# Folding the forward sequence transform of a spectral block about the middle of each tile's rows

## The chip, the cores and the metric

The kernel runs on one core of a Trainium2 chip. A core has five engines that each work through their own instructions in program order: TensorE (PE) multiplies matrices, VectorE (DVE), ScalarE (ACT) and GpSimd (POOL) work element by element, and SyncE (SP) mainly starts transfers. Transfers are also started by ACT and POOL. The metric is the device time of one execution in microseconds, the median of several runs; smaller is better. What is profiled is one execution on the chip.

## The reference

The input x is (1, 2048, 1024): S = 2048 positions and D = 1024 channels. The layer-normed x goes two ways, and the results are combined:

```python
def _A_ref(x, w_r, w_i):
    X = rfft2(x, axes=(-2, -1))
    X = X * (w_r + 1j * w_i)            # (2048, 513)
    return irfft2(X, (S, D), axes=(-2, -1))

def _B_ref(x, w1, w2):                  # w1 (1024, 3584), w2 (3584, 1024)
    h = _silu(einsum("bsd,df->bsf", x, w1))
    return einsum("bsf,fd->bsd", h, w2)

xn = _layernorm(x)
return x + _A_ref(xn, w_r, w_i) * _silu(_B_ref(xn, w1, w2))
```

## The kernel before

**Numbers.** Every product is made of float16 halves: a value is scaled and split into a high half (`high`, on ACT) and the rest (`low`, on DVE), and three matmuls (high by high, high by low, low by high) add up in PSUM.

**Two streams on PE.** The feed-forward network fills PE: 112 chunks of 24 matmuls (`pa`, line 466, 128x512 each) for the first product, then 56 chunks of 42 (`pb`, lines 549 to 551) for the second, in which seven products of halved size stand for the whole. After each `pa` chunk and each half of a `pb` chunk, `work()` lets one or more steps of a list of background jobs run; the spectral path is cut into such steps. An estimated clock for PE and one for DVE decide how many steps run, so that DVE stays near PE. The order on every engine is fixed when the program is built.

**The spectral path.** In order: `ln_gen` (layer norm), `fd_gen(c)` for c = 0 to 3 (the transform over D for the rows s = 4a + c, then a radix step over S), a switch of memory pools, `f_gen` (forward transform over S, the product with W, the first inverse radix step), a second switch, and `i_gen(c)` for c in the order 1, 3, 0, 2 (the inverse over S and D). The jobs up to the first switch are forced to their end when 15 `pa` chunks are left. A value `s` of the column sums (line 266) scales each pair of w1 blocks: PE multiplies the maxima `m1b`, which POOL casts to bfloat16 (line 290), with a tile of ones, DVE makes the scale `rs` out of it, and ACT and DVE split w1 with that.

**fd_gen, second half.** `vt` (named `V` in the trace) holds the transform over D of one c. For each j of four column blocks DVE adds and subtracts (`Rb`, `Rd`, lines 900 and 901) and makes the radix step (`radix4`, lines 244 to 247) into `Ro`; a sum `total` (line 909, called `vt` in the trace) is added; ACT and DVE split both into `Rs` (lines 884, 886, 889, 890), and SP stores them two chunks later to the DRAM tiles `vd[j]` (512 KB) and `vs[j]` (128 KB). One j is one step; the steps end two after the fourth.

**f_gen.** For 16 units u = (q, j), SP loads `vq` out of `vd[j]` (line 966, 512 KB), the weights `wq`, and for q = 2, 3 `vs`. `kq` holds the twiddle planes of a q, three for each c (cosine and both signs of the sine, or the three of a three-product complex multiplication), 768 KB; it is loaded by POOL for q = 0 and by ACT else. `mat(u)` is the product on PE, called `fx` in the trace: for q = 0, 1, in each of 12 groups, one 128x256 matmul and two of 128x128 (lines 1001 to 1003); for q = 2, 3, 36 of 128x128 (line 994) in two PSUM tiles, and DVE then adds the planes (two adds). Then DVE makes the radix step, the product with W and the next radix step.

**i_gen.** Per c, products over S (`iu`), radix or mirror steps on DVE, products back over D (`id`, line 1372), and on DVE the rows of s, `rows` (lines 1385 to 1419). The end of the kernel adds the pieces: `pl` (lines 618 and 619), times s, plus x (lines 633 and 634), out by SP; `fx` on SP is there the load of x rows, not the product.

**Queues.** SP carries nearly all loads and stores, in order. A pool switch (`close`) writes out all deferred stores, and the first tiles in the freed memory wait for everything that used it.

Of the kernel before, what the change touches and what calls it, by code (L numbers as in the profile page):

```python
# [14 lines left out]
I32 = mybir.dt.int32  # L15
AF = mybir.ActivationFunctionType
# [11 lines left out]
THREE = (2, 3)  # L28
# [9 lines left out]
RH = math.sqrt(0.5)  # L38
EPS = 1e-5
# [8 lines left out]
def make_constants():  # L48
# [9 lines left out]
    ca = np.stack(_halves(ca, 2.0**14), 1)  # L58

    q = np.arange(4)[:, None, None, None]  # L60
    a = np.arange(128)[None, :, None, None]
    c = np.arange(4)[None, None, :, None]
    m1 = np.arange(128)[None, None, None, :]
    th = 2 * np.pi * (((4 * a + c) * (4 * m1 + q)) % 2048) / 2048
    k = np.stack([-np.sin(th), np.cos(th), np.sin(th)], 3)
    k[list(THREE)] = np.stack([np.cos(th), np.sin(th) - np.cos(th), -np.sin(th) - np.cos(th)], 3)[list(THREE)]
    kc = np.stack(_halves(k, 2.0**14), 3).reshape(4, 128, 3072)
# [5 lines left out]
    for c in (0, 2):  # L73
        th = 2 * np.pi * (((4 * a + c) * (4 * row + q)) % 2048) / 2048
# [3 lines left out]
        if c == 0:  # L78
            re[..., 0:64], re[..., 64:127], re[..., 127], re[..., 128] = co[..., near], si[..., far], -si[..., 64], co[..., 64]
            im[..., 0], im[..., 1], im[..., 2:65], im[..., 65:129] = co[..., 64], si[..., 64], -si[..., far], co[..., near]  # L80
# [8 lines left out]
    for c in (1, 3):  # L89
        th = 2 * np.pi * (((4 * a + c) * (8 * half + 4 * e + q)) % 2048) / 2048  # L90
# [32 lines left out]
    tw = np.tile(tw[None], (128, 1)).astype(np.float32)  # L123
# [9 lines left out]
def spectral_ffn(ctx, tc, x, w_r, w_i, w1, w2, ca, kc, ci, tw, pm, out):  # L133
    nc = tc.nc
# [5 lines left out]
    kf = [kc[q][:, 0:3072].rearrange("a (c h t m) -> a c h t m", c=4, h=2, t=3) for q in range(4)]  # L140
    ki = [kc[c][:, 3072:5136] for c in range(4)]
# [12 lines left out]
    vs = [dp.tile([128, len(THREE), 4, 2, 128], F16, name=f"vs{j}") for j in range(4)]  # L154
# [12 lines left out]
    ones = cp.tile([128, 128], F32, name="ones")  # L167
    unit = cp.tile([128, 128], BF16, name="unit")
# [64 lines left out]
    def radix4(sign, b, d, o):  # L233
# [9 lines left out]
        sw = d[:, 1, ::-1]  # L243
        sub(o[:, 0:2], b[:, 0], b[:, 1], op=OP.add)
        sub(o[:, 4:6], b[:, 0], b[:, 1], op=OP.subtract)
        sub(pick(plus), d[:, 0], sw, op=OP.add)
        sub(pick(minus), d[:, 0], sw, op=OP.subtract)
# [568 lines left out]
    def fd_gen(c):  # L816
# [77 lines left out]
        for j in range(4):  # L894
            sl = slice(128 * j, 128 * j + 128)
            if j:
                high_r(j - 1)
# [818 lines left out]
```

## Time and profile before

| | |
|---|---|
| median of 3 runs | 1224.8 us (1223.97 to 1225.43) |
| span of the profiled execution | 1222.1 us, 19140 instructions |
| TensorE clock granted | 1.00 throughout |
| spectral forward part on the chip | radix steps of c = 0 from 142 us, of c = 3 to 523 us; `fx` from 551.5 us |

The profile's page gives for each engine its busy time and its share of the span. The views used below are the instructions in time order on an engine (start, duration, line, operation, output and inputs, and in brackets the idle time before and what ended it), a table of busy time per stretch of the span, and the list of transfers (count, size, median time from issue to landing). The span is 2.7 us shorter than the median of the runs.

### The profile page before, as it was taken

To read this page: it belongs to the slowest core of one execution; us is meant where nothing else is said; L and a number is where in the kernel's file an instruction comes from. 1 tells how busy PE (TensorE), PEld (TensorE's weight loads), DVE (VectorE), ACT (ScalarE), POOL (GpSimd) and SP (SyncE) were. 2 spreads that over 40 slices of the span, in tenths; PEclk is the share of its full clock that TensorE was granted. 3 is DMA by queue.
4 is the path that set the end of the run, shared out by engine and by line. 5 is a ranking of instruction groups with operands and counts; after the bars stand their busy time and mean duration, and the time that the engine had idled before them with its cause. 6 is when DMAs were issued, how large, how long until landed. Compare 5 with 4: busy or idle time off the path is not lost.

```text
span 1222.1 us, 19140 instructions
## 1 busy us (share of the span) xinstructions
PE 1211.3 (99%) x6992; PEld 615.4 (50%) x6992; DVE 1004.2 (82%) x2007; ACT 494.0 (40%) x670; POOL 139.9 (11%) x255
## 2 busy tenths in 40 slices
PE   8999999999999999999999999999999999999998
PEld 5544445445444444445445555554555555555545
DVE  7778997898798798968968989996378876897766
ACT  6775553455375654533433322131132322333212
POOL 3320100002010000201101121143101111000000
PEclk9999999999999999999999999999999999999999
DMA  8787585747678978479998999977979999997677
GB/s 252 186 197 187 165 257 178 207 137 206 188 259 272 316 239 282 147 244 207 184 280 294 247 253 244 306 231 251 281 199 327 262 353 291 318 362 253 230 252 273
DMA packets 285055, 299.98 MB, mean 245 GB/s; under 512 B 48928, under 2 KB 211744, under 8 KB 284576
## 3 DMA queue, kind: packets, MB, share of 16 engines
q1 hardware_dynamic: 264944, 239.95, 67.1%
q10 hardware_dynamic: 15840, 50.67, 11.9%
q0 software_dynamic: 4176, 8.13, 3.6%
q8 instruction: 55, 0.90, 0.3%
q14 instruction: 40, 0.33, 0.1%
HBM read 188.05 MB, written 104.35 MB: 239 GB/s over the span
## 4 chain that ended last, share of the span: by engine, by line
PE 83%; DVE 6%; ACT 2%; DMA 2%; issue 1%; SPq 0%; DVEq 0%; ACTq 0%; POOL 0%
PE pa L466 34%; PE pb L550 14%; PE pb L549 14%; PE pb L551 14%; PE id L1372 2%; PE fx L994 1%; DMA ws<-wd 1%; ACT xp L750 1%; PE iu L1290 1%; PE iu L1282 1%; DVE wd L383 1%; PE fx L1001 1%; DVE hr L504 1%; DVE hoone L260 1%; PE fx L1003 0%
## 5 line engine op out<-in xcount | busy, mean ns | idle before, releaser
L466 PE MATMUL pa<-xnT,w 128*128 128x512 f16 x2688 | 584.3, 379 | 1.3 <-ACT w L257 0.7
L466 PEld LDWEIGHTS <-w 128*128 128x128 f16 x2688 | 261.2, 98 | 312.5 <-issue 1.0
L549 PE MATMUL pb<-w,ht 128*128 128x512 f16 (+2 forms) x812 | 300.4, 372 | 0.0
L550 PE MATMUL pb<-w,ht 128*128 128x512 f16 (+2 forms) x812 | 300.4, 372 | 0.0
L551 PE MATMUL pb<-w,ht 128*128 128x512 f16 (+2 forms) x812 | 300.3, 372 | 0.0
L551 PEld LDWEIGHTS <-ht 128*128 128x128 f16 x812 | 79.4, 98 | 91.0
L549 PEld LDWEIGHTS <-ht 128*128 128x128 f16 x812 | 79.5, 98 | 87.0
L550 PEld LDWEIGHTS <-ht 128*128 128x128 f16 x812 | 79.4, 98 | 86.8
L475 ACT ACTIVATE h<-pa,s 128x512 f32<-128x512 f32 x112 | 75.4, 676 | 75.8 <-PE pa L466 58.5
L257 ACT ACTIVATE w<-jr,sc 128x512 f16<-128x512 f32 x98 | 68.3, 714 | 71.5 <-DMA jr<-in_B_w_dram 40.1
L260 DVE SCALAR_TENSOR_TENSOR w<-jr,sc,w 128x512 f16<-128x512 f32 x98 | 72.0, 745 | 16.8 <-ACT w L257 16.8
L257 ACT ACTIVATE hosum<-hr,hs 128x1536 f16<-128x1536 f32 x28 | 44.0, 1573 | 87.7 <-DVE hr L505 45.6
L260 DVE SCALAR_TENSOR_TENSOR hoone<-h,hs,hoone 128x2048 f16<-128x2048 f32 x28 | 65.6, 2344 | 7.3 <-ACT hoone L257 7.3
L257 ACT ACTIVATE hoone<-h,hs 128x2048 f16<-128x2048 f32 x28 | 55.8, 1994 | 29.3 <-issue 11.0
L260 DVE SCALAR_TENSOR_TENSOR hosum<-hr,hs,hosum 128x1536 f16<-128x1536 f32 x28 | 50.7, 1812 | 1.4 <-ACT hosum L257 1.4
L504 DVE TENSOR_TENSOR hr<-h 128x1024 f32<-128x1024 f32 x28 | 34.2, 1221 | 21.5 <-ACT h L475 21.5
L1033 ACT ACTIVATE zq<-Z,zs 128x1024 f16<-128x1024 f32 x16 | 18.4, 1148 | 71.9 <-DVE Z L1124 43.0
L257 ACT ACTIVATE w<-w1r,rs 128x1024 f16<-128x1024 f32 x28 | 31.9, 1142 | 37.6 <-DVE w L260 24.3
L424 POOL DMA_DIRECT2D jr<-in_B_w_dram x28 | 24.4, 948 | 178.2 <-DMA jr<-in_B_w_dram 54.6
L642 ACT ACTIVATE pl<-pl,c 128x512 f32<-128x512 f32 (+2 forms) x28 | 17.7, 656 | 66.0 <-DVE pl L618 41.8
L1124 POOL TENSOR_TENSOR Z<-yb 128x32 f32<-128x32 f32 x32 | 15.7, 510 | 209.2 <-DVE yb L1103 209.2
L260 DVE SCALAR_TENSOR_TENSOR w<-w1r,rs,w 128x1024 f16<-128x1024 f32 x28 | 35.6, 1274 | 2.3 <-ACT w L257 2.2
(240 smaller groups left out, 1575.0 us busy)
## 6 DMA issues: line engine op xcount, KB each, us to landing
w1r<-in_B_w_dram SPq DMA_DIRECT2D x28, 512.0 KB, 6.7
hd_sum<-hosum SPq DMA_DIRECT2D x56, 256.0 KB, 2.9
hd_one<-hoone SPq DMA_DIRECT2D x56, 256.0 KB, 4.2
hd_dif<-hoone SPq DMA_DIRECT2D x56, 256.0 KB, 4.3
w2m<-in_B_w_dram SPq DMA_DIRECT2D x28, 512.0 KB, 5.9
ht<-hd_dif ACTq DMA_DIRECT2D x32, 448.0 KB, 7.7
jr<-in_B_w_dram SPq DMA_DIRECT2D x56, 256.0 KB, 7.7
ht<-hd_sum ACTq DMA_DIRECT2D x32, 448.0 KB, 5.9
```

What stands on the lines that cost most here:

```text
L257: nc.scalar.activation(hi, raw, AF.Copy, scale=scale)
L260: nc.vector.scalar_tensor_tensor(lo, raw, scale, hi, op0=OP.mult, op1=OP.subtract)
L424: nc.gpsimd.dma_start(raw[n], w2_block(*todo[n], 1), accum_op=OP.add)
L466: nc.tensor.matmul(ps, w[:, wh, d], xt[:, xh, d], start=(n == 0), stop=(n == 23))
L475: nc.scalar.activation(hq[:, 2 * (c % 2) + f % 2], ps, AF.Silu, scale=s1[:, f:f + 1])
L504: tt(sums[:, 0:2], hq[:, 0::2], hq[:, 1::2], op=OP.subtract)
L549: nc.tensor.matmul(ps, hh[:, 0], w[:, 0], start=first, stop=False)
L550: nc.tensor.matmul(ps, hh[:, 0], w[:, 1], start=False, stop=False)
L551: nc.tensor.matmul(ps, hh[:, 1], w[:, 0], start=False, stop=last)
L642: nc.scalar.activation(o, o, AF.Silu, scale=c2)
L1033: nc.scalar.activation(zqs[q][:, 0, :, 16 * j:16 * j + 16], zs_[u], AF.Copy, scale=zs)
L1372: nc.tensor.matmul(ps[:, g, cols], us[g][:, uh, 4 * r + p], C["ci"][:, ch, g, r, cols], start=(r == 0 and n == 0), stop=(r == 1 and n == 2 ...
```

## The change

The forward product over S is made with one real plane for each c. With the exponent taken relative to the row MIDDLE = 254 of each tile, row r and the row facing it have the same cosine and opposite sines. Their sum needs the cosine alone, their difference the sine alone. So the two are added and subtracted beforehand ("folded"), 64 rows carry sums and 64 differences, and one plane of cosines and sines multiplies both parts. What remains of the phase for odd c is put right after the product, with a tangent.

Constants: `kc` shrinks from 3072 to 1024 forward columns per q, `ca` gets a ninth block (`eight`), `tw` gets the tangents, the sign and the two lists of facing rows, and the matrices of the inverse are shifted by the same phase (with the roles of c = 0 and c = 2 in `mirror` exchanged, six adds in place of eight for one of them).

In `fd_gen`, `total`, its split and the `vs` tiles go. Each radix result `raw` is stored whole to DRAM (`rd`, 512 KB), and POOL reads it back with an indirect transfer, the rows in facing order, into `Rt`, one step later. Two steps later DVE folds (two instructions of 128x512) and ACT splits; one step after that DVE makes the low half; `vd` is then stored in three transfers, two of them in 256-byte pieces. A c now takes seven steps. For c = 2 and 3 the rows 63 and 127, which face themselves or the middle, are taken apart in `axis_rows`: out to DRAM and back, three small matmuls (`axp`), and 32 small stores into `vd` (line 972 of the changed kernel).

```diff
-        for j in range(4):
...
-            if j:
-                low_r(j - 1)
-            r = ap.tile([128, 8, 128], F32, name=f"Ro{c}_{j}", tag="Ro", bufs=1)
-            radix4(-1, b, d, r)
-            o[j] = r.rearrange("a (q r) k -> a q (r k)", r=2)
-            total[j] = ap.tile([128, len(THREE), 128], F32, name=f"vt{c}_{j}", tag="E", bufs=1)
...
+        def fold(j):
+            if j in asked:
+                asked[j]()
+            r, t_ = (t.rearrange("a (q r) k -> a q r k", r=2) for t in (raw.pop(j), facing.pop(j)))
+            stt, o = nc.vector.scalar_tensor_tensor, folded(j)
+            stt(o[:, :, 0], t_[:, :, 0], tws[:, 24:25], r[:, :, 0], op0=OP.mult, op1=OP.add)
+            stt(o[:, :, 1], r[:, :, 1], tws[:, 24:25], t_[:, :, 1], op0=OP.mult, op1=OP.add)
...
+        def keep(j):
+            n = 64 - c // 2
+            s_ = sp.pop(j)
+            nc.sync.dma_start(vd[j][64:64 + n, :, c], s_[64:64 + n])
+            for r in range(2):
+                nc.sync.dma_start(vd[j][0:n, :, c, :, 128 * r:128 * r + 128], s_[0:n, :, :, 128 - 128 * r:256 - 128 * r])
+
+        def face(j):
+            nc.sync.dma_start(rd[c, j], raw[j].rearrange("a m k -> a (m k)"))
+            facing[j] = ap.tile([128, 8, 128], F32, name=f"Rt{c}_{j}", tag="L0", bufs=2)
...
+                    nc.gpsimd.indirect_dma_start(
+                        facing[j].rearrange("a m k -> a (m k)"), None, rd[c, j], bass.IndirectOffsetOnAxis(ap=at, axis=0))
+
+            asked[j] = gather
+            defer(1, gather)
...
+            else:
+                low(G["out"][:, 1], G["ps"][0:64, 0:128], 2.0**-15, G["out"][:, 0])
+                for e in range(2):
+                    for j in range(4):
+                        for q in range(4):
+                            at = 32 * e + 8 * j + 2 * q
+                            nc.sync.dma_start(vd[j][64 * e + 63:64 * e + 64, q, c].rearrange("a h (r k) -> (a r) h k", r=2), G["out"][at:at + 2])
+
+        for j in range(7):
+            if c > 1 and j < 5:
+                axis_rows(j)
+            if j > 2:
+                low_r(j - 3)
...
+            if 2 <= j <= 5:
+                fold(j - 2)
+                high_r(j - 2)
+            if j < 4:
+                raw[j] = ap.tile([128, 8, 128], F32, name=f"Ro{c}_{j}", tag=("Ro", "bf")[j % 2], bufs=1)
+                radix4(-1, b[:, 0], b[:, 1], d[:, 0], d[:, 1], raw[j])
+                face(j)
+                clock["dve"] -= 0.8
             yield 3.9
-        high_r(3)
-        yield 0.5
-        low_r(3)
-        yield 1
```

In `f_gen` the `vs` loads, the three-product branch and its adds go, `kq` is 256 KB, and two instructions on DVE (`xr`, 128x256 each) put the phase in:

```diff
                 for n, (kh, vh) in enumerate(((0, 0), (0, 1), (1, 0))):
-                    nc.tensor.matmul(o, k[:, c, kh, 1], v[:, c, vh], start=(n == 0), stop=False)
-                    nc.tensor.matmul(ps[:, c, 0], k[:, c, kh, 2], v[:, c, vh, 128:256], start=False, stop=False)
-                    nc.tensor.matmul(ps[:, c, 1], k[:, c, kh, 0], v[:, c, vh, 0:128], start=False, stop=(n == 2))
+                    nc.tensor.matmul(o, k[:, c, kh], v[:, c, vh], start=(n == 0), stop=(n == 2))
...
+            ro = bp.tile([128, 2, 2, 128], F32, name=f"xr{u}", tag="xr", bufs=1)
+            for r in range(2):
+                nc.vector.scalar_tensor_tensor(
+                    ro[:, :, r], bd[:, :, 1, 1 - r], tws[:, 16 + 4 * r + q:17 + 4 * r + q], bd[:, :, 1, r], op0=OP.mult, op1=OP.add)
```

The order on the engines moves at three places. On POOL, in the radix steps of c = 0, stand before (`L_` are the tiles of the transform over D, `m1b`, `s` and `hs` the w1 scales):

```order
67 L811 MEMSET L_0_2_1319 128x8
68 L811 MEMSET L_0_3_1415 128x8
69 L290 CAST m1b<-m_226 128x2
70 L296 TENSOR_SCALAR s_229<-e_225 128x2
71 L301 TENSOR_SCALAR hs<-hs 128x1
72 L290 CAST m1b<-m_226 128x2
73 L296 TENSOR_SCALAR s_229<-e_225 128x2
74 L301 TENSOR_SCALAR hs<-hs 128x1
```

After the change the same stretch reads (`Rt_j` is the facing copy of `rd_j`):

```order
67 L829 MEMSET L_0_2_1328 128x8
68 L829 MEMSET L_0_3_1419 128x8
69 L309 CAST m1b<-m_241 128x2
70 L315 TENSOR_SCALAR s_244<-e_240 128x2
71 L320 TENSOR_SCALAR hs<-hs 128x1
72 L939 DMA Rt_0_1668<-rd_0_79,tws 128x1024
73 L939 DMA Rt_1_1716<-rd_1_80,tws 128x1024
74 L939 DMA Rt_2_1767<-rd_2_81,tws 128x1024
75 L309 CAST m1b<-m_241 128x2
76 L315 TENSOR_SCALAR s_244<-e_240 128x2
77 L320 TENSOR_SCALAR hs<-hs 128x1
78 L939 DMA Rt_3_1828<-rd_3_82,tws 128x1024
```

The second cast, which PE's next column sum needs, now stands behind three indirect transfers, each of which waits for its store to `rd` to land. For c = 1 and c = 2 a cast stands in the same way behind the transfers of j = 0 and 1.

On SP, at the switch from the forward part to `f_gen` (`vd_75` to `vd_78` are the four `vd` tiles, `jr` the first loads of w2), stand before:

```order
320 L891 DMA vd_77<-Rs_2_5185 512x1x512
321 L892 DMA vs_81<-Rs_2_5185 256x1x256
322 L498 DMA hd_one_1_99<-hoone_10_1_5226 512x1x256
323 L498 DMA hd_dif_1_91<-hoone_10_1_5226 512x1x256
324 L498 DMA hd_dif_1_93<-hoone_10_1_5226 512x1x256
325 L498 DMA hd_one_1_97<-hoone_10_1_5226 512x1x256
326 L891 DMA vd_78<-Rs_3_5233 512x1x512
327 L892 DMA vs_82<-Rs_3_5233 256x1x256
328 L966 DMA vq_5356<-vd_75 128x2048
329 L979 DMA wq_0_5358<-in_A_w_r_dram 128x4x128
330 L979 DMA wq_1_5360<-in_A_w_i_dram 128x4x128
```

and after, behind 32 small stores of the `axis_rows` of c = 3:

```order
364 L517 DMA hd_one_0_110<-hoone_11_0_5375 512x1x256
365 L928 DMA vd_76<-Rs_1_5304 252x1x512
366 L930 DMA vd_76<-Rs_1_5304 252x2x128 x2
367 L928 DMA vd_77<-Rs_2_5421 252x1x512
368 L930 DMA vd_77<-Rs_2_5421 252x2x128 x2
369 L928 DMA vd_78<-Rs_3_5457 252x1x512
370 L930 DMA vd_78<-Rs_3_5457 252x2x128 x2
371 L439 DMA jr_5519<-ws_0_156 128x512
372 L439 DMA jr_5521<-ws_1_157 128x512
373 L439 DMA jr_5523<-ws_2_158 128x512
374 L439 DMA jr_5525<-ws_3_159 128x512
375 L1044 DMA vq_5527<-vd_75 128x2048
```

The load of `vq` has come to stand behind all stores of c = 3 and behind the first four `jr`, which wait, as the first use of the freed memory, for these stores to land. On ACT the high half of the fourth `Rs` waits for the stores of the second (`vd_76`) to land, since `Rs` has two buffers. On PE the first `fx` product stands behind 5 `pa` chunks from the column sum of the last w1 pair before, and behind 8 after.

On SP at the end of the program (`pl` are the pieces of the output, `fx` the rows of x) stand before:

```order
719 L542 DMA pl_7_2_12310<-pd_7_125 128x512
720 L542 DMA pl_7_0_12312<-pd_7_109 128x512
721 L566 DMA fx_3_1_12314<-in_A_x_dram 128x512
722 L566 DMA fx_3_0_12316<-in_A_x_dram 128x512
723 L636 DMA out_dram<-pl_4_2_12176 128x512
724 L636 DMA out_dram<-pl_4_0_12178 128x512
725 L636 DMA out_dram<-pl_5_2_12241 128x512
726 L636 DMA out_dram<-pl_5_0_12243 128x512
727 L636 DMA out_dram<-pl_6_2_12302 128x512
728 L636 DMA out_dram<-pl_6_0_12304 128x512
```

and after:

```order
747 L561 DMA pl_7_2_11916<-pd_7_139 128x512
748 L561 DMA pl_7_0_11918<-pd_7_123 128x512
749 L655 DMA out_dram<-pl_4_2_11622 128x512
750 L655 DMA out_dram<-pl_4_0_11624 128x512
751 L655 DMA out_dram<-pl_5_2_11802 128x512
752 L655 DMA out_dram<-pl_5_0_11804 128x512
753 L655 DMA out_dram<-pl_6_2_11908 128x512
754 L655 DMA out_dram<-pl_6_0_11910 128x512
755 L585 DMA fx_3_1_12024<-in_A_x_dram 128x512
756 L585 DMA fx_3_0_12026<-in_A_x_dram 128x512
```

The last x rows are now asked for behind the outputs of the sixth and seventh block. On DVE the last group of lines 1385 to 1419, the rows that the final pieces need, stood before behind the second of the last eight `pb` chunks and stands after behind the seventh.

More of the change, by code (lines that the diff above doesn't have):

```diff
@@ L153, in spectral_ffn @@
     vd = [dp.tile([128, 4, 4, 2, 256], F16, name=f"vd{j}") for j in range(4)]
-    vs = [dp.tile([128, len(THREE), 4, 2, 128], F16, name=f"vs{j}") for j in range(4)]
+    rd = {(c, j): dp.tile([128, 1024], F32, name=f"rd{c}_{j}") for c in range(4) for j in range(4)}
+    axis = [dp.tile([2, 4096], F32, name=f"axis{c}") for c in range(2)]
     zd = [dp.tile([128, 4, 2, 1024], F16, name=f"zd{c}") for c in range(4)]
@@ L167, in spectral_ffn @@
     ones = cp.tile([128, 128], F32, name="ones")
+    tws = cp.tile([128, 27], F32, name="tws")
     unit = cp.tile([128, 128], BF16, name="unit")
@@ L1020, in copy @@
         def copy(u):
-            if u // 4 in THREE:
-                cps[u] = bp.tile([128, 2, 2, 2, 128], F32, name=f"xo{u}", tag="T1", bufs=1)
-                for half in range(2):
-                    nc.scalar.activation(cps[u][:, half], psx[u, half][:, :, 0:128].unsqueeze(2).broadcast_to([128, 2, 2, 128]), AF.Copy)
-                return
             cps[u] = bp.tile([128, 2, 256], F32, name=f"xc{u}", tag="xc", bufs=2)
```

225 lines of the change are left out of this document (119 added, 106 removed).

## The prediction

> **What bounds the kernel now.** First the profile's page: who is busy, and what the chain that ended last consists of.
>
> ```profile
> PE 1211.3 (99%) x6992; PEld 615.4 (50%) x6992; DVE 1004.2 (82%) x2007; ACT 494.0 (40%) x670; POOL 139.9 (11%) x255
> PE 83%; DVE 6%; ACT 2%; DMA 2%; issue 1%; SPq 0%; DVEq 0%; ACTq 0%; POOL 0%
> ```
>
> PE works 99% of the span and carries 83% of the chain. So matmul time that goes is gained at once, and any wait that reaches PE is paid in full. Next the stretches of 20 us in which the changed work lies: per row the width, then busy time of PE, PEld, DVE, ACT, POOL, the clock, the DMA share and GB/s.
>
> ```profile
> 140.00:160.00 20.00, 20.00 (x94) 9.05 (x93) 19.90 (x32) 11.68 (x15) 1.35 (x1) 1.00 0.74 207
> 260.00:280.00 20.00, 20.00 (x95) 9.07 (x94) 19.80 (x38) 10.19 (x13) 1.98 (x2) 1.00 0.34 105
> 400.00:420.00 20.00, 18.57 (x136) 10.27 (x134) 16.65 (x32) 15.30 (x22) 1.56 (x5) 1.00 0.97 308
> 500.00:520.00 20.00, 20.00 (x95) 9.04 (x94) 17.61 (x27) 6.58 (x8) 6.38 (x1) 1.00 0.71 210
> 580.00:600.00 20.00, 20.00 (x98) 9.21 (x96) 19.96 (x31) 8.95 (x12) 1.95 (x4) 1.00 0.99 199
> ```
>
> PE is full in four of the five; at 400 to 420 it loses 1.4 us. The clock is 1.00, so I change nothing for it. DVE is full beside PE in the radix steps of c = 0 and 1 and in `f_gen`: whatever makes DVE wait there has no slack to come out of.
>
> **What goes on PE.** A unit of the forward product for q = 0, 1 and one for q = 2, 3, from its first matmul to the next of the network, and the pace of the network:
>
> ```profile
> 643.71 0.27 PE L1001 MATMUL fx<-vq,kq 128*128 128x256 f16 x1
> 643.82 0.22 PE L1002 MATMUL fx<-vq,kq 128*128 128x128 f16 x1
> ...
> 646.36 0.38 PE L549 MATMUL pb<-w,ht 128*128 128x512 f16 x1
> ...
> 699.64 0.33 PE L994 MATMUL fx<-vs,kq 128*128 128x128 f16 x3
> ...
> 701.65 0.38 PE L549 MATMUL pb<-w,ht 128*128 128x512 f16 x1
> ...
> 134.76 26.06 PE L466 MATMUL pa<-xnT,w 128*128 128x512 f16 x120
> ```
>
> The first takes 646.36 - 643.71 = 2.65 us, the second 701.65 - 699.64 = 2.01. A 128x256 matmul holds PE for 643.82 - 643.71 = 0.11 us. After the change every unit is 12 of these, 1.32 us. The gain is 8 x (2.65 - 1.32) + 8 x (2.01 - 1.32) = 16.2 us, less six `axp` matmuls at 2.01 / 36 = 0.06 each: **-15.9 us**. I trust this term to half a us. The last row gives 25.9 / 5 = 5.18 us for a `pa` chunk, which I need below.
>
> DVE gets two folds per tile (two 128x512 instructions) for two smaller ones that go, and two `xr` per unit for the adds of q = 2, 3 that go; that is some 10 us over 32 places. PE is full beside DVE's 19.9, since DVE runs up to a chunk behind; I cost it at nothing, and at 0 to 7 us if that cover is gone at 560 to 620 us. The traffic grows by about 10 MB (16 stores and 16 gathers of 512 KB, less `vs` and two thirds of `kq`), beside shares of 0.34 to 0.97: nothing by itself.
>
> **What comes into PE's way: column sums.** What PE waits for is set by how long a store and a gather take. Rows for that: stores and loads (count, KB, median to landing), all transfers of `vd` (shortest, median, longest), the time that SP and POOL need for one issue (`L1074` in ns, least, median, most; `L424` mean ns), and the landing of POOL's `jr`.
>
> ```profile
> vd<-Rs SPq DMA_DIRECT2D x16, 512.0 KB, 5.7
> vq<-vd SPq DMA_DIRECT2D x16, 512.0 KB, 7.3
> jr<-in_B_w_dram POOLq DMA_DIRECT2D x28, 256.0 KB, 8.8
> ...
> DMA to landing us min/median/max: 3.2/6.1/11.5
> ...
> L498 SPq DMA_DIRECT2D hd_sum<-hosum x56: 512/609/1738, 74.9 to 641.5; - x56
> L1074 SPq DMA_DIRECT2D xsv<-in_A_w_i_dram x8: 368/458/538, 668.1 to 704.1; - x8
> L424 POOL DMA_DIRECT2D jr<-in_B_w_dram x28 | 24.4, 948 | 178.2 <-DMA jr<-in_B_w_dram 54.6 <-DVE zt L1251 37.9 <-DVE w L260 34.9
> ```
>
> The trace shows no gather. I take 5.7 us for store and gather alike (same size as `vd`), bounds 3.2 (shortest) and 8.8 (POOL's `jr`), 0.65 for an issue on SP (`hd_sum` 0.61) and 0.95 on POOL. The three places where a cast now stands behind gathers:
>
> ```profile
> 144.08 0.42 DVE L247 TENSOR_TENSOR Ro<-Rd 128x256 f32<-128x256 f32 x1
> 147.10 1.35 POOL L290 CAST m1b<-m 128x2 bf16<-128x2 f32 x1 [10.03 <-ACT junk L283]
> 160.66 0.17 PE L266 MATMUL s<-m1b,unit 128*128 128x2 bf16 x1
> 268.13 0.42 DVE L247 TENSOR_TENSOR Ro<-Rd 128x256 f32<-128x256 f32 x1
> 274.87 0.17 PE L266 MATMUL s<-m1b,unit 128*128 128x2 bf16 x1
> 394.26 0.17 PE L266 MATMUL s<-m1b,unit 128*128 128x2 bf16 x1
> 398.10 0.42 DVE L247 TENSOR_TENSOR Ro<-Rd 128x256 f32<-128x256 f32 x1
> ```
>
> c = 0: the cast was done 12 us before PE's matmul at 160.66. Now the first tile (144.5) is stored and gathered: 144.5 + 0.65 + 5.7 + 0.95 + 5.7 = 157.5. DVE stands there with fold 0, then makes the third tile (1.4 + 1.35), 160.3; store, gather issue and cast bring 160.3 + 0.65 + 5.7 + 0.95 + 0.2 = 167.8. PE waits 7 us (3 to 15 by the bounds), with the whole network queued behind the column sum. c = 1: the second tile at 268.55 gives 276.05, 1.2 us (0 to 4). c = 2: the second tile comes where the fourth was, 398.5 if DVE is as late as before; then 406.0 against 394.26, 12 us; if DVE keeps up with PE, nothing. I take 6. Together **+14 us** (3 to 31).
>
> By the Trainium skill ("SBUF — State Buffer", section "SBUF: two separate sides") GpSimd can be kept from writing descriptors by VectorE instructions that hold a port both share; a DMA of 0.62 us took 3.1 there. That would speak against gathers beside a full DVE; but POOL's issues of `jr` here took 948 ns on the mean beside a DVE at 82%, so I do not add it; by it, each gather could be some 2 us later (estimate from that page).
>
> The 32 small stores of c = 2 hold SP for 32 x 0.46 = 15 us, with w2's loads and stores behind them; that stretch already lost 1.4 us to such waits. **+2 us** (0 to 8).
>
> **The switch.** The rows of before: the last column sum and the five chunks behind it, the load of `vq`, the first `fx`, and on DVE the w1 reduction, the last tile's radix step and what follows the column sum.
>
> ```profile
> 512.01 1.22 DVE L285 TENSOR_REDUCE m1b<-w1r 128x1 bf16<-128x1024 f32 x1 [2.32 <-DMA w1r<-in_B_w_dram]
> 515.41 0.68 DVE L900 TENSOR_TENSOR Rb<-V 128x512 f32<-128x512 f32 x1
> ...
> 525.34 1.22 DVE L504 TENSOR_TENSOR hr<-h 128x1024 f32<-128x1024 f32 x1
> ...
> 533.34 1.81 DVE L260 SCALAR_TENSOR_TENSOR hosum<-hr,hs,hosum 128x1536 f16<-128x1536 f32 x1
> ...
> 525.77 25.92 PE pa L466 x120
> ...
> 535.24 0.33 SPq L966 DMA_DIRECT2D vq<-vd  x1
> ...
> 551.53 0.27 PE L1001 MATMUL fx<-vq,kq 128*128 128x256 f16 x1
> ```
>
> Before, `vq` was asked for at 535.24 and had 16 us. After, PE has 8 chunks from 525.8: 525.8 + 8 x 5.18 = 567.2 is when it wants `vq`. The way there: the first tile of c = 3 stands behind both w1 reductions, at about 520.1 (512.0, three instructions of 1.2, some 2 of short writes, 2.5 for adds and radix step). Store and gather: 533.1. On DVE then the work from 525.34 to 535.15 without its 1.8 us of waiting (8.0 us) plus two folds, two radix steps, a low half and two adds (8.0): 549.1. On SP three `hd_sum` (1.9), the 32 stores (14.7), four `hd_one` (2.6), three `vd_76` (1.9): 570.2. They land at 575.9; only then the fourth tile is split (2.3) and stored (1.9), landing at 585.8. Then four `jr` and `vq` (2.9), landing 7.3 later: 596.0. PE would wait 28.8 us, 12 with all the short ends (3.2 and 0.37), 45 with the long. While PE stands it asks for nothing, so landings move to the short end: **+20 us**.
>
> By the Trainium skill ("DMA: Bandwidth & Descriptors", section "Anatomy of one DMA — SWDGE (gpsimd) path") a DMA takes about 2.0 us plus its bytes over 436 GB/s, 3.2 us for 512 KB as an estimate. By it the wait at c = 0 would be 3 us and the one here 12; the medians of 5.7 and 7.3 say more, in a kernel that keeps its queues full.
>
> **The tail.** The end before: the last matmul and the last group of rows, the final pieces and the last load of x.
>
> ```profile
> 1163.28 0.68 DVE L1385 TENSOR_TENSOR sk<-id,sc 128x504 f32<-128x504 f32 x1 [0.38 <-ACT sk L1383]
> ...
> 1167.73 0.28 DVE L1419 SCALAR_TENSOR_TENSOR rows<-sk,spa 128x128 f32<-128x128 f32 x1
> ...
> 1213.75 0.48 DVE L633 SCALAR_TENSOR_TENSOR pl<-rows,s_sc,pl 128x256 f32<-128x256 f32 x1 [0.24 <-ACT pl L642]
> ...
> 1219.17 0.29 DVE L634 TENSOR_TENSOR pl<-pl,fx 128x128 f32<-128x128 f32 x1
> ...
> 1217.18 0.22 PE L551 MATMUL pb<-w,ht 128*128 128x128 f16 x1
> ...
> fx<-in_A_x_dram SPq DMA_DIRECT2D x32, 256.0 KB, 5.8
> ```
>
> DVE ended 2.1 us after PE (1219.46 against 1217.40), and the last rows group (4.7 us) had been done 50 us before. Now it stands one chunk (42 matmuls, 9.1 us) before PE's end E. Starting between E - 13.6 and E - 9, DVE does it, two pairs of pieces (2.9 each) and two adds (1.4): E to E + 4. SP sends two outputs and asks for x: E + 2 to E + 6, landing 3 to 5.8 later; the last pieces take 5.7 (1213.75 to 1219.46). DVE ends 10 to 17 us after E instead of 2: 8 to 15 more, 4 if it starts earlier still. **+9.5 us**.
>
> **Sum.** -15.9 + 14 + 2 + 20 + 9.5 = +29.6 on the span of 1222.1, 1251.7; the runs' median stands 2.7 above it: **1254**, slower. With every short end the sum is about +3, with the long ends beyond +60.
>
> **Rivals.**
> 1. All covers hold (not slower): the gathers land early, DVE runs ahead of the column sums, and the switch and the tail have slack that I miscounted. It decides at a store-to-gather way of less than about 8 us instead of 13, and at a `vq` landing before 567. Then only PE's gain is left: 1224.8 - 15.9 = 1209. For it speaks that PE is full now with the same kind of stores; against it the order, in which the cast stands behind the gathers.
> 2. Short ends everywhere: 3 + 0 + 12 + 4 against -15.9, about 1228, 1220 to 1232: no change, nearly.
> 3. The switch at its long end, 45 instead of 20, with 15 more on the column sums: 1282 and above, if landings lengthen with 256-byte pieces and 32 issues wait for one another.
>
> **How the numbers follow.** About 0.2% (2.4 us) is what a measurement can tell from no change. Forecast (1232 to 1282) 0.58; rival 1 (1205 to 1220) 0.22; rival 2 0.13, a third of it each way; rival 3 0.07. Faster 0.22 + 0.04 = 0.26, same 0.05, slower 0.69. The range takes in rival 1 and the forecast: 1208 to 1282; the forecast's own is 1232 to 1282.
>
> **What would show it.** Right: PE idle before L266's successors at c = 0 and 2, with POOL's cast late behind a gather; PE idle before the first `fx` for 10 us or more, ended by `vq`; DVE ending 10 us after PE. `fx` units of 1.32 us show the gain. Wrong: PE full at 160 to 180 and 550 to 590 us, a gather that lands in 3 us, or stalls at places that I did not name.

## The result, and the profile after

| | us |
|---|---|
| before, median of 4 runs | 1225.03 (1223.97 to 1225.43) |
| after, median of 4 runs | 1315.66 (1314.69 to 1318.18) |
| ratio | 1.0746, 95% interval 1.0731 to 1.0762 |
| predicted | 1254, range 1208 to 1282 |

The change costs 90.6 us. The direction was forecast; the size lies outside the range. The page of the changed kernel, with PE's clock in tenths and the shares of the chain that ended last:

```profile
PE 1212.1 (92%) x6614; PEld 604.9 (46%) x6614; DVE 1019.1 (78%) x2011; ACT 484.5 (37%) x650; POOL 159.0 (12%) x271
PEclk9999989999997979989999999999979999899998
DMA 31%; DVE 25%; PE 24%; issue 5%; SPq 5%; ACT 4%; POOL 0%; ACTq 0%; DVEq 0%; POOLq 0%
```

PE carries 24% of the chain in place of 83%. It stands idle for 1312.8 - 1212.1 = 100.7 us, before for 10.8. And although 378 matmuls are gone, it is busy as long as before, because its clock is no longer full throughout. PE's own waits (total, times, longest):

```profile
PE s L285 <- POOL m1b L309: 26.3, 3, 18.3
PE fa L821 <- ACT L L831: 16.2, 2, 13.3
PE iu L1333 <- issue: 13.9, 1, 13.9
PE iu L1341 <- DVE ub L1350: 11.8, 1, 11.8
PE pa L485 <- ACT h L494: 10.5, 2, 5.5
PE fx L1063 <- DMA vq<-vd: 2.5, 1, 2.5
```

Where they stand, in the timeline (start, duration, engine, line; in brackets the idle time ahead and what ended it): the column sum of c = 0, a gather and the column sum of c = 2, the burst of 32 small stores on SP and what it holds up, ACT's cast of the last tile of c = 3, a unit of the product, and the end.

```profile
168.23 0.16 PE L285 MATMUL s<-m1b,unit 128*128 128x2 bf16 x1 [7.58 <-POOL m1b L309]
...
425.64 0.95 POOL L939 DMA_INDIRECT Rt<-rd,tws  x1 [8.94 <-DMA rd<-Ro]
426.60 0.19 POOL L309 CAST m1b<-m 128x2 bf16<-128x2 f32 x1
426.84 0.16 PE L285 MATMUL s<-m1b,unit 128*128 128x2 bf16 x1 [18.34 <-POOL m1b L309]
...
458.34 11.89 SPq L972 DMA_DIRECT2D vd<-ao  x32
482.23 1.06 ACT L918 ACTIVATE Rs<-V 128x1024 f16<-128x1024 f32 x1 [15.03 <-DVE V L914]
486.50 0.26 PE L821 MATMUL fa<-cas,xnT 128*128 128x128 f16 x1 [13.30 <-ACT L L831]
...
616.91 1.06 ACT L918 ACTIVATE Rs<-V 128x1024 f16<-128x1024 f32 x1 [18.07 <-DMA vd<-Rs]
...
711.96 1.47 PE L1063 MATMUL fx<-vq,kq 128*128 128x256 f16 x12
713.27 0.38 PE L568 MATMUL pb<-w,ht 128*128 128x512 f16 x1
...
1299.17 0.22 PE L570 MATMUL pb<-w,ht 128*128 128x128 f16 x1
1309.69 0.29 DVE L653 TENSOR_TENSOR pl<-pl,fx 128x128 f32<-128x128 f32 x1
```

A unit of the product takes 713.27 - 711.96 = 1.31 us, as worked out (1.32). The column sum stands behind POOL's cast and a gather, as named. ACT waits 15 us for a fold, with the evictions that PE needs (ACT's copies of PE's results out of PSUM) queued behind it. At the switch ACT's cast of the last tile waits 18.1 us for stores of `vd` to land, as the prediction had it. DVE ends 10.6 us after PE.

The view that explains most splits the span at the first `fx`. Columns: stretch, width, then busy time of PE, PEld, DVE, ACT, POOL, PE's clock, DMA share, GB/s. First the kernel before:

```profile
0.00:551.50 551.50, 545.40 (x2858) 264.07 (x2859) 468.06 (x945) 301.90 (x358) 61.99 (x111) 1.00 0.74 218
551.50:1222.10 670.60, 665.90 (x4135) 351.37 (x4133) 536.11 (x1062) 192.10 (x312) 77.93 (x144) 1.00 0.90 268
```

Then the changed one:

```profile
0.00:632.90 632.90, 573.47 (x2936) 275.20 (x2937) 486.95 (x955) 303.79 (x353) 83.41 (x127) 0.96 0.73 212
632.90:1312.80 679.90, 638.63 (x3678) 329.65 (x3677) 532.12 (x1056) 180.69 (x297) 75.61 (x144) 0.97 0.86 259
```

The first `fx` comes 81.4 us later: 53.3 of it are PE's longer idle time, 15.5 the three `pa` chunks that now stand ahead of it (at 5.18 us each), and the other 12.6 are PE's busy time, which goes with the lower clock (0.96). The rest is 9.3 us longer although PE is busy 27 us less in it.

### The profile page after: what moved, and what is told of

Its sections match the earlier page's. It is cut to its first block, busy times and chain, and to the rows that moved or that the text cites. A ratio compares the mean times of both kernels' runs of the same rounds, so it can differ in the third digit from the quotient of the medians.

```text
span 1312.8 us, 18536 instructions
## 1 busy us (share of the span) xinstructions
PE 1212.1 (92%) x6614; PEld 604.9 (46%) x6614; DVE 1019.1 (78%) x2011; ACT 484.5 (37%) x650; POOL 159.0 (12%) x271
## 4 chain that ended last, share of the span: by engine, by line
DMA 31%; DVE 25%; PE 24%; issue 5%; SPq 5%; ACT 4%; POOL 0%; ACTq 0%; DVEq 0%; POOLq 0%
PE pa L485 12%; DMA jr<-in_B_w_dram 3%; PE pb L568 3%; PE pb L570 3%; PE pb L569 3%; DMA sd<-s 3%; DMA zd<-zq 2%; DMA jr<-ws 2%; DMA ht<-hd_dif 2%; SPq L517 2%; DVE w L279 2%; DMA rd<-Ro 2%; DVE hosum L279 2%; DMA wq<-in_A_w_i_dram 2%; DMA ws<-wd 2%
## 5 line engine op out<-in xcount | busy, mean ns | idle before, releaser
L485 PE MATMUL pa<-xnT,w 128*128 128x512 f16 x2688 | 593.6, 383 | 11.7 <-ACT h L494 10.5
L485 PEld LDWEIGHTS <-w 128*128 128x128 f16 x2688 | 263.8, 99 | 357.5 <-issue 51.0
L569 PEld LDWEIGHTS <-ht 128*128 128x128 f16 x812 | 79.5, 98 | 87.1 <-issue 0.3
L276 ACT ACTIVATE hoone<-h,hs 128x2048 f16<-128x2048 f32 x28 | 55.8, 1994 | 45.5 <-DVE h L528 19.5
L276 ACT ACTIVATE hosum<-hr,hs 128x1536 f16<-128x1536 f32 x28 | 44.0, 1571 | 64.2 <-DVE hr L524 45.5
L918 ACT ACTIVATE Rs<-V 128x1024 f16<-128x1024 f32 x16 | 16.9, 1057 | 124.7 <-DVE V L914 86.1
L1174 POOL TENSOR_TENSOR Z<-yb 128x32 f32<-128x32 f32 x64 | 32.6, 538 | 215.6 <-DVE yb L1153 215.6
L279 DVE SCALAR_TENSOR_TENSOR hosum<-hr,hs,hosum 128x1536 f16<-128x1536 f32 x28 | 50.8, 1814 | 3.9 <-ACT hosum L276 3.9
L939 POOL DMA_INDIRECT Rt<-rd,tws x16 | 30.0, 1878 | 176.7 <-DMA rd<-Ro 102.3
L1174 DVE TENSOR_TENSOR Z<-yb 128x128 f32<-128x128 f32 (+1 forms) x128 | 43.0, 405 | 0.0
```

Source lines behind the costliest of these rows:

```text
L276: nc.scalar.activation(hi, raw, AF.Copy, scale=scale)
L279: nc.vector.scalar_tensor_tensor(lo, raw, scale, hi, op0=OP.mult, op1=OP.subtract)
L485: nc.tensor.matmul(ps, w[:, wh, d], xt[:, xh, d], start=(n == 0), stop=(n == 23))
L569: nc.tensor.matmul(ps, hh[:, 0], w[:, 1], start=False, stop=False)
L939: nc.gpsimd.indirect_dma_start(facing[j].rearrange("a m k -> a (m k)"), None, rd[c, j], bass.IndirectOffsetOnAxis(ap=at, axis=0))
L1174: eng.tensor_tensor(Z[:, ns, pos], x0[:, :, ls], x1[:, :, ls], op=o_)
```

## The experiments

Eighteen kernels, each run once beside a run of the kernel before on the same chip (1224.0 to 1225.3 there); differences under about 2.5 us are not read, and the changed kernel's own four runs lie 3.5 apart. All start from the changed kernel unless said otherwise. "Rest" is the time from the first `fx` to the end, from each run's own profile. In the expectations `pa2_22` is a chunk of the first product and `pb3_2` one of product 3 of the second; `LEAD` is how far the planner lets its clock for DVE run ahead of that for PE (1 us), before it holds the background back.

| run | us | first fx | rest | PE busy | PE idle |
|---|---|---|---|---|---|
| before | 1225.0 | 551.5 | 670.6 | 1211.3 | 10.8 |
| e8 product only | 1214.0 | 531.1 | 681.1 | 1198.3 | 13.9 |
| e17 = e14 at e8's place | 1224.7 | 538.9 | 683.9 | 1200.4 | 22.4 |
| e15 = e8 with more lag | 1230.4 | 544.9 | 683.7 | 1199.5 | 29.1 |
| e14 = e8 with fold | 1249.3 | 567.8 | 679.7 | 1199.8 | 47.7 |
| e13 no gather, no burst | 1270.9 | 587.1 | 682.1 | 1206.4 | 62.8 |
| e3 no gather | 1289.7 | 607.6 | 680.3 | 1210.6 | 77.3 |
| e16 no axis rows | 1291.5 | 608.8 | 680.9 | 1209.9 | 79.8 |
| e18 = e5 at an earlier place | 1296.1 | 620.5 | 673.8 | 1207.2 | 87.1 |
| e5 cast on ACT, burst spread | 1298.1 | 616.4 | 679.9 | 1211.9 | 84.4 |
| e11 = e5 with LEAD 3 | 1298.3 | 594.7 | 701.8 | 1221.0 | 75.5 |
| e2 no burst | 1299.2 | 611.9 | 685.5 | 1211.7 | 85.7 |
| e1 cast on ACT | 1305.6 | 625.2 | 678.6 | 1212.9 | 90.9 |
| e12 half the fold | 1312.4 | 631.9 | 678.7 | 1211.7 | 98.9 |
| after | 1315.7 | 632.9 | 679.9 | 1212.1 | 100.7 |
| e4 pace | 1317.6 | 633.2 | 682.6 | 1218.4 | 97.4 |
| e7 pace late | 1318.3 | 635.8 | 680.7 | 1219.6 | 96.9 |
| e9 less PE work | 1320.2 | 637.8 | 680.6 | 1177.7 | 140.7 |
| e10 before, less PE work | 1233.3 | 554.3 | 677.2 | 1180.7 | 50.8 |
| e6 before, three stalls | 1273.1 | 600.7 | 670.6 | 1218.7 | 52.6 |

### First: the places where PE waits

**e1**, the cast off POOL:

```diff
-                nc.gpsimd.tensor_copy(m1b[:, sl], m1[:, sl])
+                nc.scalar.activation(m1b[:, sl], m1[:, sl], AF.Copy)
```

> The bf16 cast m1b of L309 goes from POOL to ACT, so that it no longer stands behind the gathers. Places theory (each wait has its own queue as its cause, and TensorE's clock adds about 0.2 us to each us of idle time): the 26.3 us of PE's waits for the column sums of L285 fall to 10 or less, what stays being ACT's own wait for the axis rows (8.2 us in c=2); PE busy falls by 3 to 5 us; time 1285 to 1300. Traffic theory (the 16 row stores, the 16 gathers and the 256-byte pieces slow every transfer, and the waits only show where it comes out): the wait moves from L309 to fold and its cast L918, time 1308 to 1318.

Measured: 1305.6, between the two, so a partial miss for both. PE's waits, same view as above:

```profile
PE fa L821 <- ACT L L831: 18.2, 2, 15.2
PE pa L485 <- ACT h L494: 14.6, 3, 6.4
PE s L285 <- ACT m1b L309: 10.0, 2, 7.0
```

The column sums lose 16.3 us of waits, of which 6.1 come back at `fa` and `pa`. The 7.0 that stay at c = 2 are ACT waiting 7.7 us for the load of the axis rows, ahead of the cast.

**e2**, without the burst (the loop of small stores is taken out, and `keep` stores all 64 rows of each half):

> Leaves out the 64 small stores of the axis results (32 each in c=2 and c=3), so that rows 63 and 127 of those residues hold the folded rows instead of the transformed axis. Places theory: SP is free 11.9 us earlier at 458 us and 10.8 us earlier at 597 us; the 16.2 us of PE's waits for fa fall to 4 or less and the 12.9 us at the switch to 4 to 8; the 18.3 us of the c=2 column sum and the 25.7 us of iu stay; with the clock 1288 to 1298. Traffic theory (64 stores of 2 KB are 0.04 % of the bytes): 1310 to 1318.

Measured: 1299.2, as the places theory said but for 1 us: `fa` falls to 3.4, `pa` to 5.8. Sixty-four stores of 1 KB each (not 2, as the expectation has it) cost 16.5 us.

**e3**, without the store and the gather (`facing[j] = raw[j]`):

> Leaves out the way through DRAM: no store of raw, no gather; fold's two instructions stay and read raw twice instead of raw and its mirror. Places theory: the casts no longer wait behind gathers and fold waits for nothing, but SP's two bursts, the axis rows and the late start of i_gen stay: the 26.3 us at L285 fall to 3 or less, fa stays at 10 or more, iu at 20 or more; 1270 to 1285. Traffic theory (16.8 MB less): nearly all of the 90 us goes, fa and iu fall as well to under 5 us each: 1215 to 1245.

Measured: 1289.7. The 26.3 us are gone; `fa` (17.3) and `iu` (23.9) stay. The traffic theory falls. But the kernel is still 65 us behind the one before, with no gather in it.

**e4**, a planner that runs further ahead from the product on; **e7**, the same from product 1 on:

```diff
-                if clock["dve"] > clock["pe"] + LEAD or ...
+                if clock["dve"] > clock["pe"] + LEAD + (4.0 if f_job and f_job.done else 0.0) or ...
```

> From the product stage on the planner lets the background run 4 us further ahead, so that i_gen's first matmul stands behind chunk pb2_7 as in the kernel before, not behind pb3_2. Nothing else moves. Places theory (i_gen's two stalls come from its late place): the 25.7 us of iu at L1333 and L1341 fall to 6 or less, the clock gives 3 to 5 us back; 1283 to 1298. Rival 1 (traffic: the loads are slow wherever they stand): the stalls stay, 1308 to 1320. Rival 2 (DVE is the bound of this stage): the evictions of the pb chunks come late instead, PE waits there 10 us or more, 1300 to 1318.

> As e4_pace, but the planner's 4 us of lead begin only with product 1 (chunk pb1_0), so that product 0 keeps its order. If e4's new waits for ht came from DVE work pulled into product 0: the ht waits stay at 2 us or less, iu falls from 25.7 to 16 or less, 1296 to 1306. If DVE has no time left anywhere ahead of i_gen, so that each wait taken away comes back in another place: 1310 to 1320.

Measured: 1317.6 and 1318.3. The places theory falls. e4's two rivals share the range that was met; the stalls of `iu` fall from 25.7 to 11.4, which the first did not expect, and new waits come, though not at the evictions that the second named. That DVE is the bound is not shown by it. e7 meets its second branch. PE's waits in e4:

```profile
PE pb L568 <- DMA ht<-hd_sum_d: 10.9, 1, 10.9
PE pb L568 <- DMA ht<-hd_dif: 6.5, 1, 6.5
PE iu L1341 <- DVE ub L1350: 6.2, 3, 4.8
PE iu L1333 <- DVE ub L1350: 5.2, 2, 3.2
```

The two stalls of `iu` are smaller, and waits for `ht` stand in their place: ACT issues those loads and had itself waited 9.8 us for DVE's Z. In e4 and e7, behind the first `fx`, a wait that is taken away comes back elsewhere.

**e5**, cast on ACT and the burst spread (`row(e, j)` issues four stores, deferred by 1 to 8 chunks); the output is whole:

> The bf16 cast on ACT as in e1_cast_act, and the 32 small stores of each axis result are issued four at a time in the eight chunks that follow, not in one burst; the output is whole. If the burst's 11 us on SP cause the waits (places theory): fa falls from e1's 18.2 us to 5 or less, the second wait of pa at the switch (5.95 us in e1) goes, iu keeps its 25 us; 1275 to 1286. If the stores' number matters and not where they stand on SP, or another wait takes the place at once: 1298 to 1306.

Measured: 1298.1, the pessimistic branch. `fa` falls to 11.2 only, and a wait for `vq` of 8.7 us appears ahead of the first `fx`. Spreading the stores gains 7.5 us on e1, less than half of the 16.5 that leaving them out gained on the changed kernel.

### Second: what a wait costs

**e6**, the kernel before with POOL held up at three casts (160 memsets of 128x16 ahead of each):

> The kernel before, with 160 POOL memsets of 128x16 put ahead of three of its casts m1b (columns 8, 14 and 18), some 15 to 20 us of POOL each; nothing else changes, and no DMA is added. It prices a wait of PE by itself. If the clock after a wait costs about 0.2 us for each us of idle time: with X us of idle time at L266, PE's busy time rises by 0.15 to 0.25 X and the time by 1.15 to 1.25 X (X = 40: 46 to 50 us, 1271 to 1275). If the lower clock came with the change's traffic: PE busy stays within 1 us of 1211.3 and the time rises by X alone (X = 40: 1265).

Measured: 1273.1. The page's busy times:

```profile
PE 1218.7 (96%) x6992; PEld 617.8 (49%) x6992; DVE 1004.2 (79%) x2007; ACT 496.7 (39%) x670; POOL 191.4 (15%) x738
```

PE's waits (total, times, longest):

```profile
PE s L267 <- POOL m1b L295: 43.0, 3, 19.8
```

And stretches of 2 us behind the second stall (8.4 us) and the third (19.8), with the clock third from the end:

```profile
301.00:303.00 2.00, 1.63 (x5) 0.58 (x5) 1.33 (x8) 0.63 (x1) 0.93 (x5) 0.50 0.11 35
303.00:305.00 2.00, 2.00 (x8) 0.85 (x7) 2.00 (x2) 1.77 (x3) 2.00 (x1) 0.71 0.00 0
305.00:307.00 2.00, 2.00 (x11) 0.88 (x9) 2.00 (x3) 0.00 (x0) 2.00 (x1) 1.00 0.47 139
...
400.60:402.60 2.00, 1.96 (x6) 0.74 (x6) 1.65 (x13) 0.96 (x1) 0.46 (x2) 0.50 0.03 8
...
404.60:406.60 2.00, 2.00 (x7) 0.64 (x6) 2.00 (x4) 1.60 (x1) 0.00 (x0) 0.51 0.12 43
406.60:408.60 2.00, 2.00 (x11) 0.93 (x10) 2.00 (x6) 0.40 (x1) 0.00 (x0) 1.00 0.59 219
```

43.0 us of waits (41.8 us more idle time than before) cost 49 us: PE is busy 7.4 us longer for the same matmuls, 2.5 us for each stall on the mean. Behind the third stall the clock stands at 0.50 for the 6 us up to 406.6, behind the second for some 3 us only. No transfer was added, so the wait alone does it. That is the first theory: for each us of wait 0.17 of busy time (0.15 to 0.25 forecast) and 1.14 of time (just under 1.15). By the Trainium skill ("TensorE: Matmul & The Clock Gate", Part 1) the array falls to half speed after an idle window of about 3.4 us and returns after a busy one, the windows running freely; the 0.50 agrees, and 6 us fit one window that the restart cut into and one whole; the 3 us behind the second stall are shorter than one window.

### Third: who sets the time behind the first fx

**e9** and **e10** leave out one of three matmuls in products 0 and 1, after and before:

```diff
+            if m < 2:
+                nc.tensor.matmul(ps, hh[:, 0], w[:, 1], start=False, stop=last)
+                clock["pe"] += 512 * 0.4215e-3
+                continue
             nc.tensor.matmul(ps, hh[:, 0], w[:, 1], start=False, stop=False)
             nc.tensor.matmul(ps, hh[:, 1], w[:, 0], start=False, stop=last)
```

> Leaves out the third matmul (L570) of the products 0 and 1 of the FFN, 224 matmuls of 0.2155 us, 48.3 us of PE's work in the second half; the planner is told as if they were there, so that the order stays. Background theory (from the first fx to the end the background's own chain of DVE, ACT and DMA takes 680 us: 678.6 to 685.5 in the seven runs so far with the folded order, whatever the pace, and PE's waits there are only its shadow): the time falls by 0 to 10 us, 1305 to 1316. PE theory (PE bounds and the waits of iu come on top): 1265 to 1275.

> The same 224 matmuls left out of the kernel before, whose PE is 99 % busy and takes 670.6 us from the first fx to the end. If PE alone bounds it there: 1224 - 48 = 1174 to 1180. If the background is nearly as long there too: 1195 to 1222, and what is left of the 48 us is the slack that the kernel before had behind its first fx.

Measured: 1320.2 and 1233.3. With 48 us less to do, neither kernel gets faster; the one before loses 8.7. Its waits:

```profile
PE pb L549 <- DMA ht<-hd_dif: 26.8, 5, 10.4
PE pb L549 <- DMA ht<-hd_sum_d: 5.0, 1, 5.0
PE fx L998 <- DMA vs<-vs: 4.9, 1, 4.9
```

So 99% busy did not mean that PE alone bounded the kernel: behind the first `fx` something else took just as long. Both times lie beyond the forecast of at most 1316 and 1222. The new waits go with a lower clock: leaving out 48.3 us of matmuls shortened PE's busy time in e10 by 30.6 only. Why e10's rest even grew by 6.6 us is not settled.

### Fourth: building the change up from the product

**e8** keeps the product with one plane alone; **e14** adds fold's two instructions (reading raw twice); **e15** adds to e8 only one more step between radix step and cast, six steps in place of four; **e13** is the changed kernel with neither gather nor burst; **e16** lacks the axis rows; **e12** folds half of each tile.

> Only the product with one plane is kept: it leaves out the fold, the store and gather of the mirror and the axis rows, and stores each tile's high and low rows with one DMA in the loop of four steps of before, so that the product works on rows that were not folded. If the transport and the fold are what the change loses (places theory): PE busy 1194 to 1198, PE idle 12 us or less, 1206 to 1214: the 15.9 us that were counted on. If the late start of i_gen belongs to the product stage itself (its units and their DVE work): iu waits of 15 us or more stay and the time is 1222 to 1240.

> e8_product_only plus fold's two instructions for each tile (both read raw, no mirror, no store, no gather, no axis), in the loop of four steps. The planner then gives the first fx the place of the changed kernel (behind pa2_22, six chunks or about 31 us later than in e8). Background theory (first fx plus about 680 us): first fx at 560 to 570, 1238 to 1252, with waits of iu at 15 us or more. PE theory (no wait in the forward stage, so nothing is lost by a later place): 1214 to 1222.

> e8_product_only with the cast to high and low two steps behind radix4 in place of one, six steps in place of four, and the two raw buffers of the changed kernel; PE's order is e8's. If the distance by itself makes the forward stage late: 1222 or more. If not: 1211 to 1217.

> Leaves out both the way of raw through DRAM (e3) and the burst of small stores (e2); fold's two instructions, the seven steps and the loads of the axis rows stay. If the two costs stand apart from each other: 26 and 16.5 us less than the changed kernel, 1270 to 1277, first fx at about 588. If each hides behind the other, so that both must go: more than their sum, 1225 to 1262. If the planner's later place of the product stage is the floor: not below 1285.

> Leaves out the axis rows wholly (their two stores and load, the casts, the small product and the 64 small stores), so that rows 63 and 127 of two residues stay the folded ones. e2 without the 64 stores alone was 16.5 us faster. If ACT's wait for the load of the axis rows is what makes c=2's column sum 18 us late: that wait falls to 8 or less, 1283 to 1290. If it is the gathers of c=2 alone: the wait stays at 15 or more, 1294 to 1300.

> Folds only two of the four residues of each tile (the other half of V stays as it is), so that fold's two instructions have 256 elements per partition in place of 512: 32 times 0.33 us, 10.5 us of DVE less in the forward stage, with the planner's clock kept. If DVE's work bounds the forward stage: the first fx comes 8 to 12 us earlier (621 to 625 us), 1303 to 1308. If it is bound by waits (gathers, SP's bursts, ACT): 3 us or less, 1312 to 1317.

e8: 1214.0, 11 us less than the kernel before. e14: 1249.3, 35.3 more, in the range of the background theory. The two kernels, split at their first `fx`; e8:

```profile
0.00:531.10 531.10, 525.25 (x2763) 255.04 (x2764) 447.22 (x899) 290.50 (x334) 48.97 (x111) 1.00 0.75 216
531.10:1212.20 681.10, 673.02 (x3847) 344.81 (x3845) 548.30 (x1076) 196.63 (x313) 79.23 (x144) 0.99 0.87 263
```

and e14:

```profile
0.00:567.80 567.80, 561.39 (x2931) 271.28 (x2932) 483.77 (x951) 302.45 (x349) 54.43 (x111) 1.00 0.72 207
567.80:1247.50 679.70, 638.41 (x3679) 329.94 (x3677) 531.96 (x1057) 181.03 (x297) 75.32 (x144) 0.98 0.85 259
```

Until its first `fx` PE is idle for 6.4 us in e14 and 5.9 in e8: no wait of fold's shows there. The first `fx` is 36.7 us later because the planner, which charges fold to DVE, puts it seven chunks later (2931 - 2763 = 168 matmuls of 24 to a chunk, 36 us; the expectation miscounted six). Those chunks are then missing as PE's work behind it. PE has 638 us to do there, the rest takes its 680, and the difference shows up as the stalls of `iu` (24.1 us) and as DVE's end behind PE's.

e15: 1230.4, so one more step costs 16.4 without any arithmetic. e13: 1270.9, as the sum of e2 and e3: the two costs add up. e16: 1291.5, between its branches: c = 2's column sum still waits 14.6 us of 18.3, so most of that wait was the gathers', and 3.7 went with the axis rows. Against e2, which lacks the small stores alone, e16 is 7.7 us faster. e12: 1312.4. DVE's busy time is 8.7 us less there (1010.4 against 1019.1; 10.5 were expected), and the time 3.3, within the spread of the changed kernel's runs: DVE's busy time does not set the forward stage at that place.

**e17** and **e18** give e14 and e5 the earlier place by taking fold off the planner's clock; **e11** is e5 with `LEAD` at 3.

```diff
             stt(o[:, :, 1], ...)
+            clock["dve"] -= 2 * (0.12 + 512 * 1.05e-3)
```

> e14_fold_only with fold taken off the planner's DVE clock, so that the first fx stands behind pa0_25 and i_gen's first matmul behind pb3_0, as in e8; the instructions are e14's. If e14's 35 us are the later place: first fx at 531 to 540, iu waits of 5 us or less, 1214 to 1224. If DVE has no time left for fold's 24 us: PE waits 10 us or more ahead of the first fx, 1230 to 1247.

> e5_cast_spread, whole output, with fold taken off the planner's DVE clock in the same way: first fx behind pa1_25, i_gen behind pb3_0. If the place is worth in the whole kernel what it is in e14: 1262 to 1275. If the forward stage's own chain (gather, casts, ACT) sets its end: its waits grow by as much as the later ones fall, 1286 to 1300, as with LEAD 3 in e11.

> e5_cast_spread with the planner's LEAD at 3 us for the whole program: the first fx stands behind chunk pa0_25 (in e5 behind pa2_22, in the kernel before behind pa0_27) and i_gen's first matmul behind pb2_5. If the order of emission is what makes the forward stage late: the first fx comes at 580 to 595 us and the time is 1260 to 1275. If the forward stage's own chain sets it, PE waits more before the first fx instead, which comes at 605 to 620 us, and 680 us later the program ends: 1285 to 1300.

e17: 1224.7, a little above its first branch, so 24.6 of e14's 35.3 us are the place, and some 11 are left for the arithmetic itself (20 us of DVE's busy time). e18: 1296.1, and e11 1298.3: in the whole kernel the earlier place gains nothing that can be read. e11 meets neither branch whole: its first `fx` comes at 594.7, as in the first, but the rest takes 701.8, and the time is that of the second. e18's waits:

```profile
PE fa L821 <- ACT L L831: 28.7, 2, 18.0
PE s L285 <- ACT m1b L309: 24.0, 3, 18.8
PE pa L485 <- ACT h L494: 17.3, 3, 11.3
PE iu L1337 <- DVE ub L1354: 3.8, 1, 3.8
```

The stalls of `iu` are gone, and PE waits 70 us in the forward stage in place of e5's 39 (11.2, 10.7, 8.3 and the 8.7 for `vq`): its first `fx` comes at 620.5, no earlier than e5's 616.4. With gathers, lag and axis rows that stage's own chain did not get faster. e18 is the fastest whole version of the change, 1.5% faster than the changed kernel and 5.9% slower than the kernel before; e5 and e11 lie only 2 us behind it.

## Why the prediction was wrong

The span is 61.1 us above the forecast one (1312.8 against 1251.7), and the changed kernel's own trace says where they stand. PE's busy time is 16.7 us above the forecast 1195.4 (1211.3 - 15.9), which goes with the clock. The two stalls of `iu` are 25.7 us, for which no term stood: the prediction's own sign of being wrong, a stall at a place that it did not name. The four places that it named came to 62.7 us in place of 45.5: column sums 26.3, `fa` 14.8 more than before, switch 12.9, end 8.7.

What each part of the change costs is a different question. The 90.6 us can be built up from the runs: product -11.0 (e8), fold with its later place +35.3 (e14 - e8), steps and axis rows without the burst +21.6 (e13 - e14), gathers +28.2 (e2 - e13), burst +16.5 (after - e2). The order of the ladder is a choice; with e3 in place of e2, burst and gathers are 18.8 and 26.0.

- **PE's gain, -15.9.** The matmul time was right: units take 1.31 us, and e8's PE is busy 13.0 us less. 11.0 us arrive, but not where the product stands: e8's rest is 10.5 us longer than before, and its first `fx` comes 20.4 earlier, since the planner puts it four chunks earlier (2763 matmuls ahead of it in place of 2858). That the time came out near the forecast is in part luck.
- **Fold on DVE, "I cost it at nothing, and at 0 to 7 us if that cover is gone at 560 to 620 us".** This is the step that failed. Added to the bare product, fold costs 35.3 us: 24.6 for its later place and some 11 for its arithmetic (e14, e17). DVE's busy time rose by 14.9 us, not some 10, but that is the smaller part. I looked for a wait of DVE in the rows and found it covered; e14 waits no longer ahead of its first `fx` than e8 and still loses it. What I left out is that fold moves the product stage in the order, and that the rest does not get shorter with it; the stalls of `iu` are that. The 35.3 hold for fold alone. In the whole kernel the earlier place gains 2.0 (e18 against e5) and half of the fold's arithmetic 3.3 (e12): in e18 the waits of the forward stage grow by 31 us, and the first `fx` comes no earlier than in e5.
- **"PE works 99% of the span ... So matmul time that goes is gained at once."** The second failure, under the first: true ahead of the first `fx` (e6 pays its stalls in full), false behind it (e9, e10). In 19 of the 20 profiles the rest takes 671 to 686 us, with 603 to 673 us of PE's busy time in it.
- **Steps and axis rows.** No term of their own stood for the seven steps, nor for the axis rows apart from their stores; 21.6 us. e15 shows that distance alone can cost 16.4; the axis rows were 7.7 in the changed kernel (e2 - e16).
- **Column sums +14.** Place and mechanism right (7.6 at c = 0 against 7, 0.4 against 1.2 at c = 1). c = 2 was mis-sized, 18.3 against 6.
- **32 small stores of c = 2, +2 (0 to 8).** Right place, size wrong by far: 13.3 us of wait at `fa`. With those of the switch the burst costs 16.5. SP needs 0.37 us for a store, less than the 0.46 I took; what I missed is who waits behind it: `ws`'s stores, for which DVE waits 7.7 and 3.6 us, so its fold comes late, so ACT's cast, and PE's evictions stand behind that.
- **Switch +20.** The waits at L485 and at the first `fx` sum to 12.9, the low end. ACT's wait for stores of `vd` came as worked out (18.1 us), but it reached PE through the evictions (10.5 us at L485) and only 2.5 through `vq`.
- **Tail +9.5.** DVE's end behind PE's grew from 2.1 to 10.6 us, and the span behind PE's last matmul by 8.7. But in e4 and e7 DVE ends 2 us behind PE, as before the change, and they are no faster: it was a sign of the long rest, not a cost of its own. That the number fits is luck.
- **Clock.** I changed nothing for it. PE's busy time stands 13.8 us above e8's for 6 matmuls more; e6 shows that waits alone can do this, 2.5 us each on the mean.

Open: which chain makes the rest about 680 us. Less PE work (e9, e10) and another pace (e4, e7) leave it as long; no run took DVE, ACT or DMA work away there. e11's 701.8 says that it is no fixed number: an earlier start is not always used. Open too is how much of fold's 35.3 us stays beside the other parts.

## What to carry to other kernels

An engine at 99% is the bound only if nothing else is as long: take some of its work away and see whether the time follows. Split the span where the order changes stage and compare each part's length with each engine's work in it. Where a planner sets the order, an added instruction costs its place too: read from the order what moves, and price that, even where every wait seems covered.

## What was not expected of the hardware

After a wait of 8 to 20 us the clock stood at 0.50 for 3 to 6 us, so that three stalls cost 7.4 us beyond themselves (e6); the time at 0.50 did not go by the length of the wait alone (3.4 us behind the 18.3 of c = 2 in the changed kernel, 0.51 from 426.84 to 430.24; 6 behind the 19.8 in e6). A gather's issue held POOL for 1.3 us in the median and 6.9 at most, against a median of 0.87 for `jr`, and the gather landed after 6.4 in the median, near the 5.7 assumed. A burst of 32 stores of 1 KB held SP for 11.9 us at 458 us, and sixty-four of them cost 16.5 us of the time.
